# Another order for the float64 decoding inside the first MoE: ScalarE's copy one step later, and another list of units per slot

## The chip, the cores and the metric

The kernel runs on one core of one Trainium2 chip. The metric is device time in microseconds of one execution of the whole program; lower is better. Its engines each work through a queue of their own in the order in which the program lists their instructions: PE (matrix multiplies), ACT (ScalarE), DVE (VectorE), POOL (GpSimd) and SP (SyncE, which issues most of the DMAs). Semaphores hold an instruction back until what it reads has been written and what it overwrites is no longer needed.

## The reference

Attention with a learned position bias, then a mixture of eight experts (the first MoE), then a dense two-layer network (the second MoE). The change touches only the code around the last two:

```
# first MoE: each token goes to the expert with the largest logit
for e in range(E):                                   # E = 8, D = 512, F = 1024
    h = np.maximum(x[mask] @ w1[e], 0.0)
    out[mask] = gate_w[mask, None] * (h @ w2[e])
# second MoE: 2304 tokens, d_model 512, d_ff 2048; w_in and w_out are float64
h = x @ w_in
g = np.where(h > 0.0, h, alpha * (np.exp(np.minimum(h, 0.0)) - 1.0))
return (g @ w_out).astype(np.float32)
```

The weights of the second MoE arrive as float64, a format no engine multiplies. The kernel turns each number on the chip into two float32 parts, an upper one (`hi`) and the remainder (`lo`).

## The kernel before

Every product is made of three matrix multiplies of split operands: upper by upper, upper by lower, lower by upper. So each tile that PE produces in PSUM is read twice: ACT writes the upper part (`hTh`, `xTh`, `w1h`, `w2h`) and DVE subtracts it for the lower part (`hTl`, `xTl`, `w1l`, `w2l`).

The first MoE (`moe1`) goes through slots of up to 256 tokens of one expert. `slot(i)` takes one of two paths by the number of tokens in it. The full path (`layer1`) makes four groups `j` of 24 matmuls each; after each group ACT writes `hTh` and DVE `hTl` (lines 1146 and 1147). Then PE transposes the next slot's tokens (`x_transpose`, ACT `xTh` line 1074, DVE `xTl` line 1075) and runs the second layer (`layer2`, line 1188) for both halves of 128 tokens, whose output ACT scales into `y` (line 1195). The tail path (`layer1_tail`) is the same for at most 128 tokens, with `l1t` (line 1162), ACT `xgat` (line 1165) and the transposes `tph` (line 1173). Where the next slot belongs to another expert, `first_weights` (lines 1128 to 1132) splits its `w1` out of the staging tiles `stg` (ACT line 1103, DVE line 1108) and then loads its `w2` into the same tiles; `second_weights`, in the next slot, splits that `w2` and loads the following `w1`. The slots after the seventh run only while the tokens last; the sixteenth, called LAST, always runs.

Between these, the kernel decodes the float64 weights of the second MoE in 32 blocks. `decode_stages` gives the stages of a block: the load (line 1000, on SP), `magnitude` (ACT, line 1004), `upper` (two DVE instructions, lines 1007 and 1009, then ACT's copy to `hi`, line 1011), `lower` (four DVE instructions, lines 1014 to 1019) and `store` (SP, line 1025; only blocks 0 to 15, which are `w_out` and go back to DRAM; blocks 16 to 31 are `w_in` and stay in the tiles `wi`). `decode(u)` is one unit: for an even `u` it issues the lower parts of block `u/2 - 1`, the magnitude of block `u/2` and the load of block `u/2 + 2`; for an odd `u` the store of the block before and the upper part of its own. There are 66 units, 0 to 65. `UNITS` says how many each slot gets (slots 0 to 7, then LAST), and `units[i]` spreads them over eight places of a slot: `work(0)` to `work(2)` in the first layer, `work(3)` to `work(5)` after the transposes, before the second layer's first output, and `work(6)` and `work(7)` behind that output.

All queues but POOL's in the attention are written out in program order (`manual_schedule`), so the position of a unit in this code is its position on ACT, DVE and SP.

Of the kernel before, what the change touches and what calls it, by code (L numbers as in the profile page):

```python
# [40 lines left out]
DEC_W = 3  # L41
# [5 lines left out]
KVR = (1, 1, 2, 2, 2, 2, 2, 1, 1, 1, 1)  # L47
KVA = (2, 3)
OHE = ("vvv", "gvv", "gvg", "vvv")
UNITS = (0, 12, 12, 12, 10, 8, 12, 0, 0)  # L50
LAG = 1
OBUFS = 8
ROW = 520
# [111 lines left out]
class Kernel:  # L165
# [817 lines left out]
    def decode_stages(self, b):  # L983

        nc, V = self.nc, self.nc.vector  # L990
        w = self.dec_w[b % len(self.dec_w)]
        A = self.dec_m[b % len(self.dec_m)]
        r = self.dec_s[b % len(self.dec_s)]
        n = b % 16
        hi, lo = [t[:, :, 128 * n:128 * n + 128] for t in self.wi]
        v = lambda x: x.rearrange("p (k f) -> p k f", k=4)
        h, m = w[:, :, 1], w[:, :, 0]

        def load(eng=nc.sync):
            eng.dma_start(out=w.rearrange("p c w -> p (c w)"),  # L1000
                              in_=self.a["w64"][(b + 16) % 32].bitcast(I32))

        def magnitude():
            nc.scalar.activation(out=A, in_=h.bitcast(F32), func=AF.Copy, scale=2.0 ** -112)

        def upper():
            V.tensor_scalar(out=r.bitcast(I32), in0=A.bitcast(I32), scalar1=3, scalar2=0x7FFFF000,
                            op0=ALU.logical_shift_left, op1=ALU.bitwise_and)
            V.scalar_tensor_tensor(out=A.bitcast(I32), in0=A.bitcast(I32), scalar=self.dec_c[:, 0:1],  # L1009
                                   in1=r.bitcast(I32), op0=ALU.bitwise_and, op1=ALU.bitwise_or)  # L1010
            nc.scalar.activation(out=hi, in_=v(A), func=AF.Copy)

        def lower():
            V.tensor_scalar(out=r.bitcast(I32), in0=A.bitcast(I32), scalar1=self.dec_c[:, 1:2], scalar2=None,
                            op0=ALU.bitwise_and)
            V.tensor_scalar(out=m, in0=m, scalar1=9, scalar2=None, op0=ALU.logical_shift_right)
            V.scalar_tensor_tensor(out=m, in0=h, scalar=self.dec_c[:, 2:3], in1=m,  # L1017
                                   op0=ALU.logical_shift_left, op1=ALU.bitwise_or)
            V.scalar_tensor_tensor(out=lo, in0=v(m).bitcast(U32), scalar=2.0 ** -43, in1=v(r),  # L1019
                                   op0=ALU.mult, op1=ALU.mult)  # L1020

        def store():
            if b < 16:
                for j, x in enumerate((hi, lo)):
                    nc.sync.dma_start(out=self.wo_d[j, n].rearrange("p (k f) -> p k f", k=4), in_=x.bitcast(F32))

        return load, magnitude, upper, lower, store


    def moe1(self):  # L1030
        nc, tc, a, V = self.nc, self.tc, self.a, self.nc.vector
        with ExitStack() as es:
# [178 lines left out]
            dec = [self.decode_stages(b) for b in range(32)]  # L1211

            def decode(u):
                for first, stage in ((3, 4), (2, 3), (1, 2), (0, 1), (2 - 2 * DEC_W, 0)):
                    b, odd = divmod(u - first, 2)
                    if not odd and 0 <= b < 32 and (stage > 0 or b >= DEC_W):
                        dec[b][stage]()
# [6 lines left out]

            units, n = {}, 0
            for i, w in enumerate(UNITS):
                units[i] = lambda j, n=n, w=w: [decode(u) for u in range(n, n + w) if (u - n) * 8 // w == j]
                n += w

            def slot(i):  # L1230
                kind = reg(i, 1, 2)
# [425 lines left out]
```

## Time and profile before

| | |
|---|---|
| time, median of 3 runs | 1097.73 us (1094.53 to 1100.83) |
| the profiled execution | 1093.54 us, of which 1091.9 us are the span from the first to the last instruction |
| PE busy | 1035.2 us (95% of the span) |
| DVE busy | 702.0 us (64%) |
| ACT busy | 551.5 us (51%) |
| decoding, first to last magnitude | 422.8 to 581.5 us of the span |

The attention ends at about 375 us, the first MoE runs from there to 672.8 us, and the second MoE from there to the end. A busy PE here says little by itself: the records of matmuls overlap, so a stretch with waits shows best in how long a slot takes. In the rows below, "idle before" an instruction and the name behind the arrow say how long its engine stood and whose end it waited for.

### The profile page before, as it was taken

What the parts mean: (1) busy time and instruction counts of PE and PEld (TensorE: products, weight loads), DVE (VectorE), ACT (ScalarE), POOL (GpSimd) and SP (SyncE); (2) the same over time, 40 slices, a digit from 0 to 9 for tenths busy, and PEclk for the clock granted to TensorE, in tenths of its full rate; (3) what the DMA queues carried; (4) which work ended last, traced back from release to release, by engine and by line L of the source; (5) the groups of instructions that cost most, each with busy time, mean ns of one, the idle gap of its engine ahead of it and who ended that gap; (6) DMA issues with size and microseconds to landing.
All of it is one profiled execution on the core that took longest, in us unless ns stands there. A gap on an engine that the chain in (4) does not pass through costs nothing. (4 is left out here: it accounts for less than half of the span.)

```text
span 1091.9 us, 19524 instructions
## 1 busy us (share of the span) xinstructions
PE 1035.2 (95%) x6878; PEld 906.6 (83%) x6878; DVE 702.0 (64%) x1438; ACT 551.5 (51%) x1163; POOL 276.7 (25%) x437
## 2 busy tenths in 40 slices
PE   9999998999999989899899999999999999999996
PEld 3349988889998878777787888998989989899895
DVE  7779989989999895887887712533525335253350
ACT  7779877778787733444545513432424224242240
POOL 5646536665335343111211200000000000000000
PEclk9999999999999989999999999999999999999999
DMA  9985585764656477896744824600010100100000
GB/s 230 313 249 172 157 213 154 200 163 147 191 139 173 136 161 242 251 266 211 244 164 134 280 68 165 248 36 30 11 39 3 38 30 11 39 1 20 10 11 20
DMA packets 94566, 146.58 MB, mean 134 GB/s; under 512 B 11264, under 2 KB 53328, under 8 KB 94352
## 3 DMA queue, kind: packets, MB, share of 16 engines
q1 hardware_dynamic: 88976, 127.26, 39.8%
q0 software_dynamic: 5456, 17.70, 5.3%
q8 instruction: 64, 1.05, 0.4%
q14 instruction: 70, 0.57, 0.2%
HBM read 105.36 MB, written 36.70 MB: 130 GB/s over the span
## 5 line engine op out<-in xcount | busy, mean ns | idle before, releaser
L1415 PE MATMUL l1x<-xTl,wih 128*128 128x256 f32 x576 | 163.0, 283 | 0.0
L1415 PE MATMUL l1x<-xTh,wil 128*128 128x256 f32 x576 | 163.0, 283 | 0.0
L1415 PE MATMUL l1x<-xTh,wih 128*128 128x256 f32 x576 | 163.0, 283 | 0.0
L1423 DVE SCALAR_TENSOR_TENSOR t<-e,t 128x512 f32<-128x512 f32 x72 | 49.8, 692 | 132.8 <-ACT t L1422 132.8
L450 ACT ACTIVATE e<-s,mn 128x576 f32<-128x576 f32 x144 | 106.1, 737 | 33.1 <-DVE mn L440 26.8
L1439 POOL DMA_INDIRECT out<-y,idc x18 | 17.6, 979 | 395.2 <-ACT xTh L1404 271.3
L440 DVE CUSTOM_DVE_ANT_0 s<-s,bt 128x576 f32<-128x576 f32 x144 | 108.7, 755 | 7.3 <-PE s L429 4.3
L1434 PE MATMUL l2x<-woh,gTh 128*128 128x512 f32 x288 | 112.8, 392 | 0.0
L1434 PE MATMUL l2x<-wol,gTh 128*128 128x512 f32 x288 | 112.3, 390 | 0.0
L1434 PE MATMUL l2x<-woh,gTl 128*128 128x512 f32 x288 | 112.1, 389 | 0.0
L1415 PEld LDWEIGHTS l1x<-xTl,wih 128*128 128x128 f32 x576 | 110.6, 192 | 0.4
L1415 PEld LDWEIGHTS l1x<-xTh,wih 128*128 128x128 f32 x576 | 110.6, 192 | 0.4
L1415 PEld LDWEIGHTS l1x<-xTh,wil 128*128 128x128 f32 x576 | 110.6, 192 | 0.0
L1426 ACT ACTIVATE gTh<-t 128x512 fp32r<-128x512 f32 x72 | 45.5, 632 | 111.9 <-DVE t L1424 111.9
L429 PE MATMUL s<-ks,qh 128*128 128x288 f32 x320 | 92.7, 320 | 4.5 <-ACT e L450 4.4
L494 DVE TENSOR_TENSOR el<-t,eh 128x512 fp32r<-128x512 f32 x128 | 87.4, 683 | 2.8 <-DMA xgat<-in_kT 0.7
L463 PE MATMUL t<-ident,e 128*128 128x128 f32 x576 | 86.8, 273 | 0.5 <-DVE el L494 0.5
L1438 ACT ACTIVATE y<-l2x 128x512 f32<-128x512 f32 x18 | 10.8, 598 | 142.6 <-PE l2x L1434 142.6
L1427 DVE TENSOR_TENSOR gTl<-t,gTh 128x512 fp32r<-128x512 f32 x72 | 49.8, 692 | 50.4 <-ACT gTh L1426 50.4
L1188 PE MATMUL l2m<-w2h,hTl 128*128 128x512 f32 x168 | 69.9, 416 | 10.1 <-DVE hTl L1147 10.1
L487 ACT ACTIVATE eh<-t 128x512 fp32r<-128x512 f32 x128 | 75.2, 588 | 5.8 <-PE t L463 4.2
L1188 PE MATMUL l2m<-w2h,hTh 128*128 128x512 f32 x168 | 70.5, 419 | 5.8 <-ACT hTh L1146 5.6
(248 smaller groups left out, 2510.5 us busy)
## 6 DMA issues: line engine op xcount, KB each, us to landing
bt<-bias SPq DMA_DIRECT2D x32, 576.0 KB, 5.0
stg<-in_moe_w SPq DMA_DIRECT2D x32, 512.0 KB, 4.2
dec_w<-in_w SPq DMA_DIRECT2D x32, 512.0 KB, 5.4
bias<-o SPq DMA_DIRECT2D x36, 295.5 KB, 5.0
x_d<-y SPq DMA_DIRECT2D x22, 260.0 KB, 4.1
qraw<-in_qT SPq DMA_DIRECT2D x32, 160.0 KB, 3.7
k<-ks SPq DMA_DIRECT2D x32, 144.0 KB, 4.2
bt<-bias SPq DMA_DIRECT2D x32, 144.0 KB, 5.9
```

The lines of the kernel that those rows point to most:

```text
L429: nc.tensor.matmul(out=ps[:, half, 0:288], lhsT=x, rhs=k[:, half * 288:half * 288 + 288], start=(m == 0), stop=(m == len(seq) - 1))
L440: nc.vector.tensor_tensor_reduce(out=sc, in0=sc, in1=bt[:, t, :].rearrange("p (a k) -> p a k", a=2), scale=-0.125, scalar=3.0e38, op0=ALU. ...
L450: nc.scalar.activation(out=e.rearrange("p (a k) -> p a k", a=2), in_=T["ps"][:, :, 0:288], func=AF.Exp, scale=-1.0, bias=T["mn"], accum_ou ...
L463: nc.tensor.transpose(out=tp[:, c, :], in_=e[:, 128 * c:128 * c + 128], identity=ident)
L487: nc.scalar.activation(out=d["eh", T["b"]][:, 0:4, o:o + 128], in_=T["tp"], func=AF.Copy)
L494: nc.vector.tensor_tensor(out=d["el", bb][:, 0:4, o:o + n_], in0=src, in1=d["eh", bb][:, 0:4, o:o + n_].bitcast(F32), op=ALU.subtract)
L1188: nc.tensor.matmul(out=p, lhsT=hT[h][:, k, 128 * t:128 * t + 128], rhs=w2[wt][:, k, :], start=(k == 0 and h == wt), stop=(k == 7 and wt == 1))
L1415: nc.tensor.matmul(out=p[:, m, :], lhsT=wi[wt][:, k, ms], rhs=xT[x][:, k, :], start=(n == 0), stop=(n == 11))
L1423: V.scalar_tensor_tensor(out=t, in0=e, scalar=1.0, in1=t, op0=ALU.add, op1=ALU.mult)
L1426: nc.scalar.activation(out=gT[0][:, gs, :], in_=t, func=AF.Copy)
L1427: V.tensor_tensor(out=gT[1][:, gs, :], in0=t, in1=gT[0][:, gs, :].bitcast(F32), op=ALU.subtract)
L1434: nc.tensor.matmul(out=p, lhsT=gT[h][:, k, 128 * t:128 * t + 128], rhs=wo[wt][:, k, :], start=(n == 0), stop=(n == 47))
```

## The change

Two things. ACT's copy to `hi` leaves the stage `upper` and becomes a stage `high` of its own, which runs one unit later, ahead of `lower` of the same block. And the number of units is no longer spread evenly over eight places: `UNITS` lists them place by place. Slots 1 to 3 get 11 units where they had 12, slot 4 gets 8 (10), slot 5 8 (8), slot 6 10 (12), slot 7 4 (0) and LAST 3 (0). No slot has units at the places 6 and 7 any more.

```diff
-UNITS = (0, 12, 12, 12, 10, 8, 12, 0, 0)
+UNITS = ((), (2, 2, 1, 2, 2, 2), (2, 2, 1, 2, 2, 2), (2, 2, 1, 2, 2, 2), (2, 2, 0, 2, 1, 1), (0, 1, 1, 2, 2, 2),
+         (2, 2, 0, 2, 2, 2), (0, 2, 0, 2), (0, 1, 0, 2))
...
                                    in1=r.bitcast(I32), op0=ALU.bitwise_and, op1=ALU.bitwise_or)
+
+        def high():
             nc.scalar.activation(out=hi, in_=v(A), func=AF.Copy)
...
-        return load, magnitude, upper, lower, store
+        return load, magnitude, upper, high, lower, store
...
-                for first, stage in ((3, 4), (2, 3), (1, 2), (0, 1), (2 - 2 * DEC_W, 0)):
+                for first, stage in ((3, 5), (2, 3), (2, 4), (1, 2), (0, 1), (2 - 2 * DEC_W, 0)):
...
-                units[i] = lambda j, n=n, w=w: [decode(u) for u in range(n, n + w) if (u - n) * 8 // w == j]
-                n += w
+                units[i] = lambda j, n=n, w=w: [decode(n + sum(w[:j]) + u) for u in range(w[j] if j < len(w) else 0)]
+                n += sum(w)
```

How the queues move is shown at two places. First ACT's queue of the kernel before, from the end of slot 2 into slot 3. `wih` is the copy to `hi`, `dec_m` the magnitude, `y` an output of the second layer, and `hTh` the first group of slot 3.

```order
L1011 ACTIVATE wih<-dec_m_5738 128x4x128
L1004 ACTIVATE dec_m_5739<-dec_w_5736 128x512
L1011 ACTIVATE wih<-dec_m_5739 128x4x128
L1195 ACTIVATE y_70<-l2m,gate 128x512
L1048 TENSOR_LOAD tabi x2
L1255 COMPARE_AND_BRANCH
L1146 ACTIVATE hTh<-l_7198 128x512
```

The same place of the changed kernel, whose lines are numbered four higher:

```order
L1015 ACTIVATE wih<-dec_m_5737 128x4x128
L1006 ACTIVATE dec_m_5738<-dec_w_5735 128x512
L1259 UNCONDITIONAL_BRANCH
L1199 ACTIVATE y_70<-l2m,gate 128x512
L1052 TENSOR_LOAD tabi x2
L1259 COMPARE_AND_BRANCH
L1150 ACTIVATE hTh<-l_7206 128x512
```

Before, the copy of the block whose upper part DVE has last in its queue stands ahead of `y` and `hTh`; now the copy ahead of them is that of the block before, and the last upper part's copy comes in slot 3.

Second, DVE's queue in slot 7, tail path, of the kernel before, from the second `hTl` to the branch at the slot's end:

```order
L1177 TENSOR_TENSOR hTl<-tph,hTh 128x4x128
L1075 TENSOR_TENSOR xTl<-tp,xTh 128x4x128 x2
L1118 COMPARE_AND_BRANCH
L1108 TENSOR_TENSOR w1l<-stg_5726,w1h 128x4x256
L1108 TENSOR_TENSOR w1l<-stg_5727,w1h 128x4x256
L1108 TENSOR_TENSOR w1l<-stg_5728,w1h 128x4x256
L1108 TENSOR_TENSOR w1l<-stg_5729,w1h 128x4x256
L1118 UNCONDITIONAL_BRANCH x2
L1048 TENSOR_LOAD tabi
```

and of the changed kernel, from `xTl` to the third of the four `w1l`:

```order
L1079 TENSOR_TENSOR xTl<-tp,xTh 128x4x128 x2
L1009 TENSOR_SCALAR dec_s_5741<-dec_m_5739 128x512
L1011 SCALAR_TENSOR_TENSOR dec_m_5739<-dec_m_5739,dec_c,dec_s_5741 128x512
L1018 TENSOR_SCALAR dec_s_5741<-dec_m_5739,dec_c 128x512
L1020 TENSOR_SCALAR dec_w_5736<-dec_w_5736 128x512
L1021 SCALAR_TENSOR_TENSOR dec_w_5736<-dec_w_5736,dec_c 128x512
L1023 SCALAR_TENSOR_TENSOR wil<-dec_w_5736,dec_s_5741 128x4x128
L1122 COMPARE_AND_BRANCH
L1112 TENSOR_TENSOR w1l<-stg_5726,w1h 128x4x256
L1112 TENSOR_TENSOR w1l<-stg_5727,w1h 128x4x256
L1112 TENSOR_TENSOR w1l<-stg_5728,w1h 128x4x256
```

One decoded block now stands between the transposed tokens and the split of the next expert's first weights; a second one follows the split, ahead of the next slot's work.

## Rows read from the trace of the kernel before

**Rows 1.** The page, busy time of each engine.
```profile
PE 1035.2 (95%) x6878; PEld 906.6 (83%) x6878; DVE 702.0 (64%) x1438; ACT 551.5 (51%) x1163; POOL 276.7 (25%) x437
```

**Rows 2.** Slots 1 to 7 and LAST by windows: start:end, us, busy us of each engine (instructions).
```profile
core 0: us, PE busy (x) PEld busy (x) DVE busy (x) ACT busy (x) POOL busy (x), PEclk, DMA share, GB/s
419.00:442.17 23.17, 23.17 (x154) 21.25 (x153) 17.45 (x31) 9.88 (x17) 5.33 (x8) 1.00 0.74 229
442.17:470.97 28.80, 25.55 (x153) 22.29 (x152) 23.74 (x42) 11.63 (x20) 3.61 (x7) 0.94 0.87 269
470.97:497.32 26.35, 24.01 (x154) 21.09 (x152) 22.41 (x41) 10.22 (x19) 3.41 (x7) 1.00 0.90 265
497.32:526.01 28.69, 26.01 (x153) 22.03 (x152) 23.20 (x37) 13.42 (x21) 4.86 (x7) 0.94 0.61 181
526.01:557.21 31.20, 25.78 (x153) 21.90 (x152) 27.10 (x45) 14.62 (x24) 5.13 (x7) 0.95 0.71 245
557.21:581.69 24.48, 23.72 (x154) 21.17 (x153) 20.61 (x37) 10.21 (x19) 1.89 (x5) 1.00 0.35 123
581.69:594.98 13.29, 13.04 (x65) 10.69 (x64) 11.01 (x17) 9.24 (x14) 3.92 (x6) 1.00 0.31 102
...
659.20:672.77 13.57, 13.27 (x66) 10.92 (x67) 2.58 (x4) 3.26 (x6) 0.56 (x3) 1.00 0.44 140
```

**Rows 3.** PE in slot 5: start, us, instruction, [idle before, releaser].
```profile
544.67 0.80 PE L1188 MATMUL l2m<-w2h,hTl 128*128 128x512 f32 x1 [3.20 <-DVE hTl L1147]
```

**Rows 4.** Who waited for whom: us in total, times, longest.
```profile
ACT wih L1011 <- DVE dec_m L1009: 80.1, 30, 4.8
```

**Rows 5.** DVE in order of time, from slot 2's first hTl to slot 3's.
```profile
449.53 0.69 DVE L1147 SCALAR_TENSOR_TENSOR hTl<-l,hTh 128x512 fp32r<-128x512 f32 x1 [2.81 <-ACTq L1118]
...
455.02 0.69 DVE L1147 SCALAR_TENSOR_TENSOR hTl<-l,hTh 128x512 fp32r<-128x512 f32 x1 [1.18 <-ACT hTh L1146]
...
477.45 0.69 DVE L1147 SCALAR_TENSOR_TENSOR hTl<-l,hTh 128x512 fp32r<-128x512 f32 x1 [1.76 <-ACTq L1118]
```

**Rows 6.** ACT at the end of slot 2.
```profile
472.77 0.66 ACT L1004 ACTIVATE dec_m<-dec_w 128x512 f32<-128x512 f32 x1
475.73 0.64 ACT L1011 ACTIVATE wih<-dec_m 128x512 fp32r<-128x512 f32 x1 [2.29 <-DVE dec_m L1009]
```

**Rows 7.** DVE in slot 3: a hTl, a pair of xTl, then decoding.
```profile
489.89 0.68 DVE L1147 SCALAR_TENSOR_TENSOR hTl<-l,hTh 128x512 fp32r<-128x512 f32 x1
490.49 1.28 DVE L1075 TENSOR_TENSOR xTl<-tp,xTh 128x512 fp32r<-128x512 f32 x2
491.92 0.45 DVE L1007 TENSOR_SCALAR dec_s<-dec_m 128x512 int32<-128x512 int32 x1
...
495.45 0.42 DVE L1007 TENSOR_SCALAR dec_s<-dec_m 128x512 int32<-128x512 int32 x1
...
496.69 0.49 DVE L1014 TENSOR_SCALAR dec_s<-dec_m,dec_c 128x512 int32<-128x512 int32 x1
...
498.94 0.42 DVE L1007 TENSOR_SCALAR dec_s<-dec_m 128x512 int32<-128x512 int32 x1
```

**Rows 8.** DVE in slots 7 and 8.
```profile
590.12 1.28 DVE L1075 TENSOR_TENSOR xTl<-tp,xTh 128x512 fp32r<-128x512 f32 x2
591.50 4.63 DVE L1108 TENSOR_TENSOR w1l<-stg,w1h 128x1024 fp32r<-128x1024 f32 x4
599.76 2.36 DVE L1108 TENSOR_TENSOR w2l<-stg,w2h 128x1024 fp32r<-128x1024 f32 x2 [3.63 <-ACT w2h L1103]
```

**Rows 9.** ACT in slot 8.
```profile
598.03 0.60 ACT L1165 ACTIVATE xgat<-l1t 128x512 f32<-128x512 f32 x1 [2.02 <-PE l1t L1162]
```

**Rows 10.** PE's longest wait from 580 to 640 us: total, times, longest.
```profile
PE l2m L1188 <- DVE hTl L1147: 0.9, 1, 0.9
```

**Rows 11.** SP in slot 3, and a window of slot 2.
```profile
500.39 2.52 SPq L1025 DMA_DIRECT2D wo_d<-wih  x1
...
467.00:473.00 6.00, 6.00 (x37) 5.30 (x36) 5.79 (x11) 2.56 (x5) 0.00 (x0) 1.00 1.00 271
```

## Prediction

> **What bounds the kernel now.** I read the page first. PE is busy 95% of the span and DVE 64% [rows 1], so a gain has to come from places where PE stands, and the share of DVE says nothing of a single stage. The table by slots comes next, cut where PE starts a slot's first layer [rows 2]. Slot 1 has nothing to wait for: 23.17 us, PE busy from end to end. So this is what a full slot costs PE. Slots 2 to 6 have the same matmuls and take 28.80, 26.35, 28.69, 31.20 and 24.48 us, together 139.52 us against 5 x 23.17 = 115.85. The difference, 23.7 us, is all that a better order inside these slots can give. In the same rows DVE works 20.6 to 27.1 us per slot; the stage hangs on DVE, and on whom DVE waits for.
>
> Then PE's own waits: in slot 5 the second layer stood 3.20 us for a `hTl` of DVE [rows 3], and behind such a wait the clock fell: the granted clock of slots 2, 4 and 5 is 0.94 or 0.95, that of the others 1.00 [rows 2]. Last, who holds DVE up. ACT stood 80.1 us in front of `wih`, 30 times, for the upper part that DVE had just been given [rows 4]. ACT's queue is in order, so the next `hTh` stands behind that copy, and DVE's `hTl` waits for the `hTh`. DVE loses 1.18 us so in the middle of slot 2 and 1.76 us at the start of slot 3 [rows 5], where ACT's copy is free 2.29 us late [rows 6].
>
> **The change, part by part.** First DVE's prices [rows 7]. A `hTl` holds it 0.60 us (489.89 to 490.49), the pair of `xTl` 1.43 (to 491.92), an upper part 1.24 (495.45 to 496.69), the lower part 2.25 (to 498.94): one block, two units, 3.5 us. A full slot's own work is 4 x 0.60 + 1.43 = 3.83 us. For the kernel before this gives 6 x 3.5 + 3.83 + 1.18 + 1.76 = 27.8 us in slot 2; the two `hTl` at 449.53 and 477.45 are 27.9 apart [rows 5], so the list is complete to 0.1 us.
>
> *High one unit later.* It is the same instruction at the same price on ACT, which is half idle. The copy then waits for an upper part that lies a whole unit back on DVE, and where a place of the slot ends with an odd unit nothing of ACT waits at all. Where a place holds an odd and then an even unit, the copy still waits for DVE, but DVE then has 2.25 us of lower part to do, longer than copy and magnitude (0.64 and 0.66 us [rows 6]) and a `hTh` (some 0.6, as `xgat` [rows 9]) take together. So both of DVE's stalls go, 2.9 us a slot. What is late next is DVE's own turn at the slot's start, which no row separates from the 1.76 us: between 0 and 1.76, and I take 0.6, since most of that wait is ACT's chain of copy, `y` and `hTh`.
>
> *The new list.* DVE's work by slot: slot 2 has 6 upper and 5 lower parts, 18.7 + 3.8 = 22.5 us; slot 3 has 5 and 6, 19.7 + 3.8 = 23.5; slots 4 and 5 have 4 blocks, 14.0 + 3.8, and a split of weights each, 4.6 as in slot 7 [rows 8], 22.5; slot 6 has 5 blocks, 21.3. With 0.6 us per slot start that is 112.3 + 3.0 = 115.3 us for five slots, against PE's 115.85. The placement fits too: six units, 10.5 us, follow the transposes and run beside the second layer, and only five or fewer stand between the four `hTl`, of which the last is asked for when the second layer has three quarters of its first half behind it. PE is the bound again, with no margin: slot 3 is 1 us over its share, and in slot 5 the second split still stands ahead of three `hTl`. For these, and for loads that come late in slots 2 and 3, I add 2.6 us to the floor: 118.5 us. Gain 139.5 - 118.5 = 21.0 us. Bounds: 23.7 if no wait is left, and 12.2 if all stalls stay as they are and only the 7 units (3.5 blocks) that leave these slots count.
>
> *Slot 7's four units.* These cost. Slot 7 splits the first weights of the next expert, then loads its second ones into the freed staging tiles; slots 8 and 9 change experts again, and PE waits at most 0.9 us in that stretch [rows 10], so weights and PE run level and a delay is passed on. The first two units stand between `xTl` and the split: DVE's `w1l`, at 591.50 before [rows 8], starts 3.5 us later, and ACT's `w1h` with it, behind a copy that waits for DVE. The other two come after the split, in the old count at 591.5 + 3.5 + 4.6 = 599.6 us. ACT's copy there waits for an upper part until 600.9, and behind it stand copy, magnitude and `y`, some 0.65 us each, so the `xgat` of slot 8, at 598.03 before [rows 9], moves to 602.8. The `w2l` of slot 8 had 3.63 us of idle time before it [rows 8], which takes up part of the second block; it moves by 5 as `xgat` does. So slot 8 and the loads behind it come 5 us late. Bounds: 0, if the next weights had slack the rows don't show, and 7.0, both blocks in full.
>
> *LAST's three units* are one block, 3.5 us of DVE behind `xTl`. Before, DVE has only 2.58 us of work in that whole slot [rows 2], and the second MoE needs block 31 only in the last eighth of its first layer. I take 0; bound 3.5.
>
> Nothing of the load or store is added or taken; each DMA moves with its unit. Sum: -21.0 + 5.0 + 0 = -16.0 us. The profiled execution took 1093.5 us (span 1091.9), which would become 1077.5. It lies 4.2 us below the median of the runs shown, so against the median of 1097.7 I forecast 1081.7, **1081 us**.
>
> **The rivals.** (a) *The stalls stay.* ACT goes on holding DVE up at other places, and only the removed work counts: -12.2 + 5 = -7.2 us, 1090.5. For it: the odd-even places keep a wait of ACT for DVE. Against it: the list of DVE's time, complete to 0.1 us [rows 5 to 7], where both stalls have a named cause that goes. (b) *The DMA queues become the bound in slots 2 and 3.* They move 269 GB/s x 28.80 us = 7.7 MB in slot 2; less half a block (0.5 MB) in 23.2 us would need 310 GB/s. In six microseconds of slot 2 the share is full at 271 GB/s, and a store's issue was held 2.52 us in slot 3 [rows 11]. At 271 GB/s slot 2 takes 26.6 us, 3.4 more; slot 3, with 265 x 26.35 = 7.0 MB less the same, takes 24.0, what DVE takes anyway: -16.0 + 3.4 = -12.6, 1085.1. The Trainium skill (DMA: Bandwidth & Descriptors, Specifications) names 358 GB/s of HBM per core. By that rule 7.2 MB would take an estimated 20.1 us and this rival would fall; the full share at 271 GB/s in this trace speaks against the rule for these transfers. (c) *Slot 7's blocks are hidden*: -21, 1076.7. Against it stands only that PE and weights run level in slots 8 and 9. (d) *Slower.* Each `hTh` now stands behind a copy that waits for a whole block of DVE. If DVE falls one block (3.5 us) behind PE and stays there, PE waits that much in each of slots 2 to 6, and the clock falls behind each wait: 0.94 over 28.8 us is a loss of 1.7. Then 115.85 + 5 x 5.2 = 141.9 us, 2.3 above now, and slot 7 costs its full 7.0: +9.3, 1107. It decides from where DVE's work exceeds PE's 23.17 us in slot after slot; by the list above only slot 3 does, by 0.9.
>
> **How the numbers follow.** Chances: forecast 0.60 (1076 to 1084), (a) 0.14, (b) 0.12, (c) 0.08, (d) 0.06. What a measurement of this kernel can tell from no change is 0.5%, 5.5 us. The forecast, (c) and nearly all of (b) are faster than that; (a) lies on the edge, half of it within. So faster 0.86, same 0.08, slower 0.06. The forecast's bounds, -23.7 to -1.7 with all costs at their ends, are 1074 to 1096; with the spread of the runs (3 us to each side) and (a) inside I give 1071 to 1093.
>
> **What would show it.** Right: ACT's wait before the copy to `hi` falls far below 80 us in total; slots 2 to 6 take 23 to 25 us each with a granted clock of 1.00; slot 7's first matmul comes near 560 us; the stretch from there to the second MoE's first matmul grows from 91.1 us (581.69 to 672.77) to about 96 [rows 2], with PE waiting at `tph` or in the second layer of slots 8 and 9. Wrong: slots 2 and 3 with a DMA share of 1.00 and ACT waiting for `dec_w` (rival b); `hTl` still waiting for `hTh` in the full slots (a, d); a stretch after slot 7 as long as now (c), or longer by more than 7 us, where LAST's block would be found.

## The result, and the profile after

The changed kernel takes 1079.69 us (median of four runs, 1077.34 to 1081.36) against 1096.13 us of the kernel before on the same chip: ratio 0.9865, 95% interval 0.9834 to 0.9896, a gain of 16.4 us by the medians. The forecast was 1081 us, a gain of 16.0, with a range of 1071 to 1093. The profiled execution took 1077.34 us, its span 1075.7 us, 16.2 us less than before.

The instructions are as many as before [rows 1]; PE is busy 7.8 us less for the same 6878 matmuls, DVE and ACT 2 us more:

```profile
PE 1027.4 (96%) x6878; PEld 904.2 (84%) x6878; DVE 704.0 (65%) x1438; ACT 553.2 (51%) x1163; POOL 277.9 (26%) x437
```

The windows from one slot's first matmul to the next one's, slots 1 to 8 and LAST, with the columns of [rows 2] (the last one runs 0.1 us past LAST's end):

```profile
419.71:442.88 23.17, 23.17 (x153) 21.25 (x152) 17.85 (x32) 9.35 (x16) 6.12 (x13) 1.00 0.85 267
442.88:466.01 23.13, 23.13 (x153) 21.25 (x152) 21.12 (x37) 10.47 (x18) 3.42 (x7) 1.00 0.85 270
466.01:490.84 24.83, 23.76 (x153) 21.11 (x152) 21.38 (x39) 10.97 (x20) 3.91 (x7) 1.00 0.89 292
490.84:514.18 23.34, 23.34 (x153) 21.18 (x152) 21.73 (x35) 12.78 (x21) 4.23 (x7) 1.00 0.80 243
514.18:540.00 25.82, 24.04 (x153) 21.01 (x152) 21.87 (x35) 12.82 (x21) 4.07 (x7) 1.00 0.75 254
540.00:563.16 23.16, 23.16 (x153) 21.20 (x152) 21.44 (x38) 10.68 (x19) 1.39 (x5) 1.00 0.48 156
563.16:577.67 14.51, 13.49 (x65) 10.46 (x64) 11.08 (x19) 8.81 (x15) 2.89 (x3) 1.00 0.50 155
577.67:592.50 14.83, 12.05 (x50) 9.52 (x51) 13.63 (x18) 10.64 (x16) 8.26 (x11) 0.88 0.74 242
643.37:656.90 13.53, 13.23 (x65) 10.88 (x66) 5.93 (x10) 3.90 (x7) 0.56 (x3) 1.00 0.44 141
```

Slots 2, 4 and 6 now take what PE needs, 23.1 to 23.3 us, and the granted clock of slots 2 to 6 is 1.00 everywhere. Slots 2 to 6 sum to 120.28 us (139.52 before), a gain of 19.2. Slot 8, cut short in this window, lasts to 595.71 (18.04 us, before 13.53), at a granted clock of 0.88 in its first 14.8 us. From slot 7's first matmul to the second MoE's first (656.79) it is 93.63 us, before 90.92 (581.69 to 672.61): 2.7 us given back. The other 0.3 us lie ahead of slot 2 (+0.7) and behind the first MoE (-0.4).

Part of the gain is the clock. Before, the granted clock was 0.50, that is 1.2 GHz where 1.00 is 2.4, for 3.4 us each in slots 2, 4 and 5, from 462.67, 517.28 and 544.59 us on, each time from the end of a wait of PE's. The changed kernel has no such stretch in slots 2 to 6 and one in slot 8, after a wait of 1.72 us. The third of before, after the 3.20 us of [rows 3], and the one after:

```profile
544.59:548.00 3.41, 3.33 (x7) 2.12 (x8) 2.19 (x6) 2.23 (x5) 0.00 (x0) 0.50 0.95 350
```

```profile
587.27:590.68 3.41, 3.41 (x15) 3.22 (x16) 3.41 (x4) 3.41 (x6) 2.36 (x2) 0.50 0.57 155
```

At half the clock 3.4 us do the work of 1.7; by this estimate some 5 of the 19.2 us are the clock, and 1.7 of the 4.5 us that slot 8 lost.

PE's remaining waits in the full slots (start, us, instruction, [idle before, releaser]) are one in slot 3 and two in slot 5, where the longest was 3.20 us [rows 3]:

```profile
483.41 0.50 PE L1192 MATMUL l2m<-w2h,hTh 128*128 128x512 f32 x1 [0.85 <-ACT hTh L1150]
...
528.72 0.50 PE L1192 MATMUL l2m<-w2h,hTl 128*128 128x512 f32 x1 [0.52 <-DVE hTl L1151]
533.29 0.50 PE L1192 MATMUL l2m<-w2h,hTl 128*128 128x512 f32 x1 [1.20 <-DVE hTl L1151]
```

ACT's waits between 415 and 680 us (total, times, longest). The copy to `hi` still waits 67.1 us, against 80.1 [rows 4]:

```profile
ACT wih L1015 <- DVE dec_m L1011: 67.1, 28, 4.0
...
ACT dec_m L1006 <- DMA dec_w<-in_w: 5.4, 4, 2.1
```

What fell is DVE's wait for `hTh`, before and after, from 415 to 600 us:

```profile
DVE hTl L1147 <- ACT hTh L1146: 10.0, 8, 1.8
```

```profile
DVE hTl L1151 <- ACT hTh L1150: 1.3, 2, 0.7
```

DVE's `hTl`, the four of slot 2 and the first of slot 3. The wait in the middle of slot 2 is gone; the one at slot 3's start is not, 1.91 us where it was 1.76 [rows 5]:

```profile
446.80 0.69 DVE L1151 SCALAR_TENSOR_TENSOR hTl<-l,hTh 128x512 fp32r<-128x512 f32 x1 [1.05 <-ACTq L1122]
451.14 0.68 DVE L1151 SCALAR_TENSOR_TENSOR hTl<-l,hTh 128x512 fp32r<-128x512 f32 x1
455.24 0.68 DVE L1151 SCALAR_TENSOR_TENSOR hTl<-l,hTh 128x512 fp32r<-128x512 f32 x1
456.96 0.68 DVE L1151 SCALAR_TENSOR_TENSOR hTl<-l,hTh 128x512 fp32r<-128x512 f32 x1
...
472.19 0.69 DVE L1151 SCALAR_TENSOR_TENSOR hTl<-l,hTh 128x512 fp32r<-128x512 f32 x1 [1.91 <-ACT dec_m L1006]
```

ACT just before that last one. What holds it is no longer the copy, but a block that comes late from DRAM, and two `y` in a row:

```profile
466.18 0.64 ACT L1015 ACTIVATE wih<-dec_m 128x512 fp32r<-128x512 f32 x1 [1.49 <-DVE dec_m L1011]
468.36 0.67 ACT L1006 ACTIVATE dec_m<-dec_w 128x512 f32<-128x512 f32 x1 [1.54 <-DMA dec_w<-in_w]
468.94 1.26 ACT L1199 ACTIVATE y<-l2m,gate 128x512 f32<-128x512 f32 x2
470.08 0.60 ACT L1150 ACTIVATE hTh<-l 128x512 fp32r<-128x512 f32 x1
```

In slots 7 and 8 ACT and then DVE show the two blocks. Counted from slot 7's first matmul, `w1l` starts 13.56 us in (before 9.81), `xgat` 21.03 (16.34) and `w2l` 22.76 (18.07) [rows 8, 9]: 3.8, 4.7 and 4.7 us later.

```profile
575.57 3.90 ACT L1107 ACTIVATE w1h<-stg 128x1024 fp32r<-128x1024 f32 x4 [0.39 <-SPq L1122]
582.52 0.64 ACT L1015 ACTIVATE wih<-dec_m 128x512 fp32r<-128x512 f32 x1 [3.05 <-DVE dec_m L1011]
...
584.19 0.60 ACT L1169 ACTIVATE xgat<-l1t 128x512 f32<-128x512 f32 x1
```

```profile
576.72 4.63 DVE L1112 TENSOR_TENSOR w1l<-stg,w1h 128x1024 fp32r<-128x1024 f32 x4 [0.41 <-ACT w1h L1107]
...
585.92 2.36 DVE L1112 TENSOR_TENSOR w2l<-stg,w2h 128x1024 fp32r<-128x1024 f32 x2 [1.06 <-ACT w2h L1107]
```

One thing the prediction did not look at: SP's queue. The two `y` of a slot go to the same DRAM tensor, and the second store waits on SP until the first has landed (`DMA x_d<-y` in the rows below). SP's waits of that kind from 415 to 600 us, before and after:

```profile
SPq L1199 <- DMA x_d<-y: 5.7, 5, 2.1
```

```profile
SPq L1203 <- DMA x_d<-y: 24.3, 6, 4.6
```

Before, decoding at places 6 and 7 stood between the two `y`. In the new list nothing does, and both come at once. SP in slot 3 after (the pair of stores, then the next load of a block), and ACT, where that load's block is awaited ahead of the `hTh` for which PE waits 0.85 us:

```profile
470.51 6.04 SPq L1203 DMA_DIRECT2D x_d<-y  x2
478.50 0.34 SPq L1002 DMA_DIRECT2D dec_w<-in_w  x1
```

```profile
482.20 0.67 ACT L1006 ACTIVATE dec_m<-dec_w 128x512 f32<-128x512 f32 x1 [1.06 <-DMA dec_w<-in_w]
482.78 0.58 ACT L1150 ACTIVATE hTh<-l 128x512 fp32r<-128x512 f32 x1
```

### The profile page after: what moved, and what is told of

It is laid out like the page before. It is cut to its first block, busy times and chain, and to the rows that moved or that the text cites. A ratio compares the mean times of both kernels' runs of the same rounds, so it can differ in the third digit from the quotient of the medians.

```text
span 1075.7 us, 19524 instructions
## 1 busy us (share of the span) xinstructions
PE 1027.4 (96%) x6878; PEld 904.2 (84%) x6878; DVE 704.0 (65%) x1438; ACT 553.2 (51%) x1163; POOL 277.9 (26%) x437
## 3 DMA queue, kind: packets, MB, share of 16 engines
q8 instruction: 64, 1.05, 0.4%
## 5 line engine op out<-in xcount | busy, mean ns | idle before, releaser
L431 PE MATMUL s<-ks,ql 128*128 128x288 f32 x256 | 72.5, 297 | 0.0
L465 PEld LDWEIGHTS t<-ident,e 128*128 128x128 f32 x576 | 71.1, 141 | 0.7 <-ACT eh L489 0.6
```

Of the source, the lines that this page charges most:

```text
L431: nc.tensor.matmul(out=ps[:, half, 0:288], lhsT=x, rhs=k[:, half * 288:half * 288 + 288], start=(m == 0), stop=(m == len(seq) - 1))
L465: nc.tensor.transpose(out=tp[:, c, :], in_=e[:, 128 * c:128 * c + 128], identity=ident)
```

## The experiments

All in one table: us per slot from the first matmul of each slot, as above; "2 to 6" their sum; "7 on" from slot 7's first matmul to the second MoE's first. The instructions ahead of slot 1 are the same in all of these kernels, and yet slot 1 begins between 414.35 and 423.98 us in these profiles. So the medians tell kernels a few us apart only roughly, and the slots, most of which come out within 0.8 us in the repeats, tell where. Slot 8 differs by 1.1 us between the two profiles of e7: one has 3.4 us at a granted clock of 0.50 there, the other none.

| kernel | median us | ratio (95%) | 2 | 3 | 4 | 5 | 6 | 2 to 6 | 7 | 8 | 9 | 10 | LAST | 7 on |
|---|---|---|---|---|---|---|---|---|---|---|---|---|---|---|
| before | 1096.13 | 1 | 28.80 | 26.35 | 28.69 | 31.21 | 24.47 | 139.52 | 13.29 | 13.53 | 25.73 | 24.96 | 13.41 | 90.92 |
| changed | 1079.69 | 0.9865 (0.9834-0.9896) | 23.13 | 24.83 | 23.34 | 25.82 | 23.16 | 120.28 | 14.51 | 18.04 | 23.13 | 24.53 | 13.42 | 93.63 |
| e1_copy_only | 1080.22 | 0.9879 (0.9846-0.9912) | 23.44 | 25.53 | 23.14 | 30.33 | 23.14 | 125.58 | 13.29 | 13.51 | 25.09 | 25.11 | 13.44 | 90.44 |
| e2_list_only | 1084.31 | 0.9919 (0.9886-0.9951) | 24.79 | 30.31 | 23.14 | 25.98 | 23.14 | 127.36 | 14.54 | 18.04 | 23.17 | 24.76 | 13.63 | 94.14 |
| e3_counts_only | 1084.40 | 0.9922 (0.9895-0.9949) | 27.21 | 27.17 | 23.14 | 29.28 | 23.14 | 129.94 | 13.65 | 17.63 | 23.17 | 24.90 | 13.87 | 93.22 |
| e4_slot7_to_last | 1080.56 | 0.9897 (0.9866-0.9928) | 23.14 | 24.62 | 23.44 | 25.31 | 23.16 | 119.67 | 14.69 | 16.16 | 23.68 | 24.89 | 17.77 | 97.19 |
| c0_changed | 1077.09 | 0.9868 (0.9839-0.9897) | 23.13 | 25.17 | 23.50 | 25.13 | 23.15 | 120.08 | 14.56 | 17.88 | 23.14 | 24.75 | 13.43 | 93.76 |
| e5_last_pair_behind | 1073.80 | 0.9826 (0.9797-0.9856) | 23.13 | 23.19 | 23.18 | 25.11 | 23.14 | 117.75 | 14.01 | 17.97 | 23.36 | 24.58 | 13.54 | 93.46 |
| e6_slot5_late | 1078.07 | 0.9871 (0.9843-0.9899) | 23.14 | 25.52 | 23.44 | 23.50 | 25.51 | 121.11 | 14.60 | 16.78 | 23.17 | 24.65 | 13.41 | 92.61 |
| e7_both | 1070.07 | 0.9813 (0.9779-0.9847) | 23.13 | 23.51 | 23.19 | 23.16 | 24.01 | 117.00 | 14.00 | 17.09 | 23.17 | 24.57 | 13.41 | 92.24 |
| e7_again | 1072.81 | 0.9809 (0.9783-0.9836) | 23.13 | 23.43 | 23.13 | 23.67 | 24.78 | 118.14 | 14.02 | 18.23 | 23.14 | 24.49 | 13.43 | 93.31 |
| e8_second_block | 1075.47 | 0.9843 (0.9813-0.9874) | 25.13 | 24.29 | 23.60 | 23.16 | 24.08 | 120.26 | 14.01 | 15.22 | 25.95 | 24.45 | 13.42 | 93.05 |
| e9_slot7_free | 1073.91 | 0.9825 (0.9799-0.9851) | 25.42 | 24.81 | 23.18 | 23.17 | 24.18 | 120.76 | 13.30 | 13.50 | 23.85 | 24.50 | 14.18 | 89.33 |
| e10_early_copy | 1079.44 | 0.9879 (0.9850-0.9908) | 25.28 | 27.89 | 23.71 | 23.17 | 24.20 | 124.25 | 14.01 | 17.06 | 23.56 | 25.05 | 13.40 | 93.08 |

e1 to e4 shared runs of the kernel before with a median of 1092.37 us, c0 to e7_both 1091.79, e7_again to e10 1091.62.

### The two halves of the change

**e1_copy_only**: `high` as in the change, the old list spread evenly.

```diff
-UNITS = ((), (2, 2, 1, 2, 2, 2), ...
+UNITS = (0, 12, 12, 12, 10, 8, 12, 0, 0)
```

> Only the copy is moved; the list of units is the old one (12, 12, 12, 10, 8, 12, spread over eight places). Theory (both parts count, the copy ends DVE's two stalls of 2.9 us a slot): the stalls are what is left of the 21.0 us when the 12.2 us of removed work are taken off, 8.8 us, so about 1087 us against 1096 of before, with slots 2 and 3 at 25 to 26 us. Rival 1 (the copy's place is worth nothing, since ACT still waits 67.1 us for upper parts in the changed kernel): 1096. Rival 2 (the copy is the whole gain of slots 2 to 6): 1096 - 19 = 1077, since slot 7 is spared.

Slots 2 to 6 fell by 13.9 us, much more than the 8.8 of the theory and less than the 19.2 of the second rival, since slot 5 hardly moved; the first rival falls. The total, 0.9879, lies between the theory and the second rival. The windows of slots 2 to 6:

```profile
444.91:468.35 23.44, 23.43 (x153) 21.17 (x152) 21.79 (x39) 10.48 (x19) 3.66 (x7) 1.00 0.99 308
468.35:493.88 25.53, 23.73 (x153) 21.17 (x152) 23.87 (x43) 11.53 (x21) 4.26 (x7) 1.00 0.95 291
493.88:517.02 23.14, 23.14 (x154) 21.25 (x152) 22.09 (x36) 13.29 (x22) 5.67 (x7) 1.00 0.70 216
517.02:547.35 30.33, 26.61 (x154) 23.25 (x153) 28.85 (x48) 15.66 (x25) 6.10 (x7) 0.89 0.74 249
547.35:570.49 23.14, 23.14 (x154) 21.25 (x153) 20.33 (x36) 10.18 (x18) 1.32 (x5) 1.00 0.40 144
```

With all 12 units slot 2 takes 23.44 us and slot 4 23.14: the sum of DVE's work in a slot, 24.8 us by the prediction's prices, was no floor there. DVE did 21.8 of it within the slot; the rest ran into later ones. What is left over comes due in slot 5, where DVE also has the split, is busy 28.85 us with 48 instructions (35 in the changed kernel), and PE waits 1.05 and 2.67 us and runs at half the clock for 6.8 us from about the end of the second wait.

**e2_list_only**: the copy directly behind its upper part, the new list.

```diff
         def upper():
             ...
+            nc.scalar.activation(out=hi, in_=v(A), func=AF.Copy)
         def high():
-            nc.scalar.activation(out=hi, in_=v(A), func=AF.Copy)
+            pass
```

> The new list of units, but the copy to hi directly behind its upper part as before. Theory (both parts count): the stalls come back where a place holds an even and then an odd unit (slot 2's second half, slot 3's first half, slot 6), so 3 to 9 us above the changed kernel: 1083 to 1089. Rival (the new list begins most places with an odd unit, where the copy's old and new place are the same on the queue; so the list alone does it): 1080, slots 2 and 6 at 23.2 us each.

7.1 us more than the changed kernel in slots 2 to 6, all of it in slots 2 and 3 (1.7 and 5.5), the other slots to 0.2 us as there. That is the theory in size, but the places are not quite the ones it names: the copy stands elsewhere where an odd unit is the last before other work. A place with an even and then an odd unit is one such case, where other work follows it; another is an odd unit with a place to itself, as in slot 2, between the third `hTl` and the fourth. There the copy holds the fourth `hTh`, DVE stands 1.18 us as it did before in mid-slot [rows 5], and PE waits 0.79 us:

```profile
459.44 0.69 DVE L1152 SCALAR_TENSOR_TENSOR hTl<-l,hTh 128x512 fp32r<-128x512 f32 x1 [1.18 <-ACT hTh L1151]
```

Slot 6 has no such place, so the expectation of a stall there was wrong. ACT in slot 3 (the copy for DVE, then `hTh`), and PE's wait for it, from about the end of which the granted clock is 0.50 for 6.8 us, by the estimate above 3.4 of slot 3's 5.5 us:

```profile
484.69 0.63 ACT L1013 ACTIVATE wih<-dec_m 128x512 fp32r<-128x512 f32 x1 [3.58 <-DVE dec_m L1011]
485.22 0.58 ACT L1151 ACTIVATE hTh<-l 128x512 fp32r<-128x512 f32 x1
```

```profile
485.85 0.80 PE L1193 MATMUL l2m<-w2h,hTh 128*128 128x512 f32 x1 [3.09 <-ACT hTh L1151]
```

**e3_counts_only**: new numbers per slot, evenly spread, the copy early.

```diff
+UNITS = (0, 11, 11, 11, 8, 8, 10, 4, 3)
```

> Only the numbers per slot are the new ones (11, 11, 11, 8, 8, 10, 4, 3); the units are spread evenly over eight places and the copy stands where it was. Theory (removed work counts 12.2 us, slot 7's units cost the 2.5 us that the changed kernel shows): 1096 - 9.7 = 1086. Rival 1 (only the sum per slot matters, DVE being below PE's 23.17 us in each slot): 1080, as the changed kernel. Rival 2 (places matter, counts don't: the units between the hTl hold PE's second layer up as before): 1093 to 1096.

Slots 2 to 6 gained 9.6 us (theory 12.2), 7 on lost 2.3. Total 0.9922, 8.5 us of 1092.4, near the theory's 9.7. Slots 2, 3 and 5 still wait, so sums per slot are not all. (The execution profiled here took 1090.85 us, 6.5 above the median, and its slot 1 begins 5.0 us later than that of the kernel before.) The parts do not add up: 9.6 for counts, 12.2 for the list (counts and places), 13.9 for the copy, 19.2 for list and copy. List and copy overlap by 6.9 us: in part they remove the same waits.

### What slot 7 costs

**e4_slot7_to_last**: slot 7's four units in LAST.

```diff
-         (2, 2, 0, 2, 2, 2), (0, 2, 0, 2), (0, 1, 0, 2))
+         (2, 2, 0, 2, 2, 2), (), (0, 2, 2, 3))
```

> The changed kernel with slot 7's four units moved into LAST, which then has seven. Theory (slot 7's blocks delay the splits of the next weights by 2.5 us net, and LAST's DVE, busy 5.9 of 13.5 us, takes another 7 us beside PE): slot 7 to the second MoE 91 us again instead of 93.6, 1077 us. Rival 1 (LAST's blocks then stand in front of DVE's first work of the second MoE, or its first layer wants block 30 before it is there): 1080 to 1084. Rival 2 (the 2.5 us come from the loads of the weights, which start no earlier, and not from the units): 1080 as now.

This is not the theory: slot 7 takes 14.69 us without any unit in it. LAST pays 4.35 us for seven units, PE waiting 2.19 us at 656.27 to read a `hTl`, with DVE's decoding (L1020) named as what it waited for, and the total is no better (0.9897). The second rival comes nearest: the loads start no earlier (below). What slot 7 waits for, ACT names:

```profile
573.94 3.90 ACT L1107 ACTIVATE w1h<-stg 128x1024 fp32r<-128x1024 f32 x4 [3.87 <-SPq L1122]
```

By this row ACT's `w1h` waits for SP to reach the same branch (L1122). SP had issued the first of the two `y` stores at 566.46 and the second only at 571.48. So there were two causes for slot 7's lateness, and taking one away left the other.

**c0_changed** is the changed kernel again, beside the next three.

> The changed kernel itself, on the same chip as the next three, to compare them with. All theories: 0.985 to 0.988 of the kernel before; slots 2 to 6 23.1, 24.8, 23.3, 25.8 and 23.2 us, slots 7 and 8 14.5 and 18.0.

As expected; slots 3 and 5 differ by 0.3 and 0.7 us from the first profile.

**e5_last_pair_behind**: the last units of slots 1 to 6 behind the first `y` (slots 1 to 3 shown).

```diff
-(2, 2, 1, 2, 2, 2)
+(2, 2, 1, 2, 2, 0, 2)
```

> The changed kernel with the last units of slots 1 to 6 moved from place 5 to place 6, behind the first of the two outputs y. Theory (in the changed kernel both y of a slot come at once behind the decoding, the second one's store waits on SP for the first to land, 24.3 us in six slots, and SP is late for the next load in slot 3 and for the branch in slot 7, on which ACT's w1h waits): SP's wait falls below 10 us, slot 3 takes under 24.2 us instead of 24.8, slots 7 and 8 together under 31 instead of 32.5; 2 to 3 us less than the changed kernel. Rival 1 (slots 7 and 8 are late because of slot 7's own four units): 14.5 and 18.0 stay, no difference. Rival 2 (units between the two y hold up the second y and the hTh behind it): slots 2 to 6 a microsecond longer each, 3 to 5 us more than the changed kernel.

SP's wait fell to 9.6 us and slot 3 to 23.19, both as the theory has it; 3.3 us less than c0 by the medians, 2.6 by the slots from 2 on. The total alone does not show it, its interval overlaps c0's. ACT's wait for `dec_w` up to 600 us fell from 5.4 us in the changed kernel (5.9 in c0) to 0.2. Slots 7 and 8 gained only 0.5 together, so for these the first rival is right: `w1h` no longer waits for SP there (575.22, no idle time before it), and the units decide. SP's waits, and SP in slot 3, where a load now goes between the two stores:

```profile
SPq L1203 <- DMA x_d<-y: 9.6, 6, 2.4
```

```profile
469.82 0.47 SPq L1203 DMA_DIRECT2D x_d<-y  x1
471.43 0.33 SPq L1002 DMA_DIRECT2D dec_w<-in_w  x1
...
475.77 0.36 SPq L1203 DMA_DIRECT2D x_d<-y  x1
```

**e6_slot5_late** and **e7_both**:

```diff
-(0, 1, 1, 2, 2, 2)
+(0, 0, 0, 2, 2, 4)       # e6
+(0, 0, 0, 2, 2, 0, 4)    # e7, with e5's other places
```

> The changed kernel with slot 5's two units of the places 1 and 2 moved to place 5, so that nothing of the decoding stands between the split of the second weights and the last three hTl. Theory (in slot 5 the split of 4.7 us and these units stand ahead of the hTl for which PE waits 0.52 and 1.20 us): slot 5 takes 23.2 to 24.2 us instead of 25.8, slot 6 stays under 23.6; 1.5 to 2.5 us less than the changed kernel. Rival (the hTl are late because ACT's w2h waits 2.83 us for SP's queue, so the units don't matter): slot 5 25 us or more, no difference.

Slot 5 fell to 23.50 us, so the two units between the split and the `hTl` were most of its price (ACT's `w2h` still waits 2.36 us there, so the rival falls), but slot 6 rose to 25.51: four units ahead of the `y` pair moved the delay on. No gain.

> Both of these edits. Theory: they add up, 4 to 5 us less than the changed kernel, about 1075 us. Rival (four units in one place at the end of slot 5 hold the last y and slot 6's first hTh, or the stores now collide with the loads): 0 to 2 us less.

With the four units behind the first `y`, slot 5 takes 23.16 and slot 6 24.01: 3.1 us less than c0 in slots 2 to 6. The medians say 7.0 us on this chip; the slots account for 4.6, and for 2.4 in the repeat.

> e7_both once more, on the same chip as the next three. All theories: 0.979 to 0.984 of the kernel before; slots 7 and 8 14.0 and 17.1 us, slots 9 and 10 23.2 and 24.6.

0.9809 (0.9783 to 0.9836): the lowest ratio, below the kernel before by 1.9% and below the changed kernel by about half a per cent. The intervals of e5 and e9 overlap it, so that it is the best of them is not shown.

**e8_second_block** and **e9_slot7_free**, from e7:

```diff
-(2, 2, 1, 2, 2, 0, 2)  slot 1;  (0, 2, 0, 2) slot 7;  (0, 1, 0, 2) LAST
+(2, 2, 2, 2, 2, 0, 3)  slot 1;  (0, 2)       slot 7;  (0, 1, 0, 2) LAST    # e8
+(2, 2, 2, 2, 2, 0, 3)  slot 1;  ()           slot 7;  (0, 2, 0, 3) LAST    # e9
```

> e7_both with slot 7's second two units (place 3, behind the split of the weights) moved to slot 1, which then has 13, as (2, 2, 2, 2, 2, 0, 3); the units of all later slots come two earlier, with the same places. Theory (slot 8's xgat stands on ACT behind a copy that waits 3.1 us for the block behind the split, and PE waits 0.5 and 1.7 us for it): slot 8 falls from 17.1 to 14 to 15 us, slots 9 and 10, which wait for loads again, give 1 to 2 us of it back, the sum is 1 to 1.5 us under e7; slot 1 stays at 23.2. Rival 1 (slot 8 is late because of w1l, which stands behind the first block): slot 8 stays at 16.5 to 17. Rival 2 (two more units in slot 1 put DVE behind, and slot 2 takes 1 to 3 us more): above e7.

Slot 8 fell by 3.0 us against e7_again, and slot 9 rose by 2.8: over the stretch the second block costs nothing that the repeats could tell (93.05 against 93.31 and 92.24). Slot 2 rose by 2 us (the second rival), so slots 2 to 6 take 2.1 us more than in e7_again; in the total the intervals overlap.

> e7_both with no unit in slot 7: two more in slot 1 (13), two more in LAST (5, as (0, 2, 0, 3)). Theory: slots 7 and 8 take 13.3 and 13.5 us as in the kernel before, slots 9 and 10 25.1 each, so that of the 3.7 to 4.3 us that slots 7 and 8 win about 2.5 are given back; LAST, which cost 4.3 us with seven units and nothing with three, costs 1 to 2 with five. About the same as e7. Rival (slot 7's blocks cost 5 us net as predicted): 3 us or more under e7.

Slots 7 and 8 are back at 13.3 and 13.5 us, and 7 on takes 89.33, 4.0 us under e7_again although LAST pays 0.75 for five units. For that stretch the rival is right: without the first block, and with the stores apart as in e7, it is 2.9 to 4.0 us shorter. The windows of slots 7 to 9:

```profile
564.53:577.83 13.30, 13.05 (x66) 10.70 (x64) 10.37 (x16) 9.18 (x14) 3.84 (x6) 1.00 0.46 145
577.83:591.33 13.50, 13.25 (x65) 10.62 (x64) 9.34 (x10) 8.83 (x13) 5.33 (x8) 1.00 0.87 290
591.33:615.18 23.85, 23.46 (x153) 21.17 (x152) 12.26 (x13) 11.49 (x15) 4.44 (x8) 1.00 0.81 280
```

The time is lost again in slots 2 and 3 (25.42 and 24.81), as slot 2 was in e8, so the total is not under e7's.

One number tells these kernels apart in two groups: when the first of the four loads behind the `w1l` of slot 7 is issued, from slot 7's first matmul. SP in e9, 11.0 us in:

```profile
575.54 3.78 SPq L1097 DMA_DIRECT2D stg<-in_moe_w  x4
```

It is 11.1 us in the kernel before and in e1, 14.8 in the changed kernel (units and SP), 15.0 in e4 (SP alone), 14.3 in e5, e7_again and e8 (units alone), 11.0 in e9 (neither). From there to slot 10's first matmul it is 39.5 to 41.5 us in all eight, and in the other six as well, whatever slot 8 does between. Inside a group, this spread of 2 us decides.

**e10_early_copy**: e7 with the edit of e2.

> e7_both with the copy to hi back behind its upper part. Theory (the copy's place matters only where an even and then an odd unit share a place: slot 2's second half, slot 3's first half, now also the pair at place 6 of slots 2 and 3): slots 2 and 3 together 5 to 8 us longer, the other slots as in e7. Rival (with the y pair apart the copy's place no longer matters): no difference.

Slots 2 and 3 take 53.17 us instead of 46.56, 6.6 more, the others as in e7 to 0.6 us: the theory. The copy's place matters in e7's list too.

## Why the prediction was right, point by point

**The bound.** Right: the gain lay in slots 2 to 6, in waits for `hTh` and `hTl`, and the clock rose with them to 1.00. 118.5 us were forecast there, 120.3 came, and slot 7's first matmul came at 563.2 instead of near 560. The allowance of 2.6 us over PE's floor was too small: 4.4 remained, nearly all in slots 3 and 5, the two that it was meant for. That the total came out to half a us is in part luck: 1.8 us too much gain here and 2.3 too much cost behind slot 7 nearly cancel.

**The high stage.** Right in kind: without it (e2, e10) the copy holds `hTh` again, 6.6 to 7.1 us in slots 2 and 3. Alone it gave 13.9 us, not the 8.8 of e1's expectation. The prediction set a slot's DVE work against PE's time slot by slot; e1 shows that work in excess of a slot can run into the next, as long as the `hTl` are served in time, and that what is left over comes due later, there in slot 5. Of the two stalls only the one in mid-slot went. At the slot's start 1.91 us stayed where 0.6 were allowed, with another cause (a late block, two `y`).

**The new list.** Right that it helps; what it is worth hangs on the copy. In slots 2 to 6 it gave 12.2 us without the copy moved (e2) and 5.3 on top of it (125.58 to 120.28), 4.5 of these in slot 5, where the half clock goes too. Behind slot 7 it costs 3.2 us on top of the copy (90.44 to 93.63). So in the whole program the copy alone does nearly all: 0.9879 in e1 against 0.9865 and 0.9868, which these intervals do not tell apart. The prediction's bound of 12.2 counts seven units, but only six leave slots 2 to 6 (10.5 us at its price); the seventh leaves slot 1, and counts as far as slot 1's excess runs into slot 2, as e8 shows it does. Slot 5's rest was placed rightly (split and units ahead of the `hTl`: e6, e7). For slot 3 the prediction named DVE's one us too much and late loads; its 1.7 us came from late loads, and e5 shows that these came from SP, which the list had left without work between the two stores.

**Slot 7's units.** The term that was off: +5.0 forecast, +2.7 measured. `w1l`, `xgat` and `w2l` came as late as forecast (3.8, 4.7, 4.7 us), and slots 7 and 8 took 5.7 us more. The step that failed is "so weights and PE run level and a delay is passed on", and with it "so slot 8 and the loads behind it come 5 us late": the loads go out right behind `w1l`, so only 3.8 late, and the second block runs beside them, which e8 shows. Slots 9 and 10, which had 25.73 and 24.96 us where a full slot needs 23.2, gave 3.0 us back; [rows 10] shows only the longest of PE's waits, not what these slots lost. Also, the units were not the only cause; SP alone makes the loads as late (e4). What the units alone cost is told by e7 against e9, both with the stores apart: 2.9 to 4.0 us, or 3.7 to 4.7 if the 0.75 that LAST pays in e9 is left out. That is nearer to 5.0 than 2.7 is, and the kernel before, with 90.92 us against 89.33 in e9, was not at its floor.

**LAST.** Right: 13.42 us against 13.41. Five units cost 0.75, seven 4.35.

**The rivals.** (a) fell: DVE's wait for `hTh` went from 10.0 to 1.3 us, and e1 and e2 show the copy's part in it. (b) fell: slot 2 took 23.13 us, e1's slot 2 moved 308 GB/s in 23.44, and from 466 to 472 us the queues moved 375 GB/s, so the full share at 271 GB/s was no ceiling. The kernel before could have told, six us of its slot 5 moved 393 GB/s:

```profile
526.00:532.00 6.00, 6.00 (x52) 5.99 (x51) 5.75 (x12) 2.36 (x4) 0.00 (x0) 1.00 1.03 393
```

The rule quoted from the Trainium skill (DMA: Bandwidth & Descriptors, Specifications), 358 GB/s for a core, was the better guide here, and in these six us the traces lie above it. Rival (c) fell by 2.7 us, (d) with slots 2 to 6.

**The signs.** The stretch behind slot 7 grew, to 93.6 us where about 96 were forecast, with PE waiting 1.72 us at `tph` in slot 8, as said; slots 2 to 6 kept to their 23 to 25 us but for slot 5 (25.8). One sign was ill chosen. ACT's wait before the copy was to fall far below 80 us; it is 67.1, or 65.0 to 600 us, and 79.1 to there in e2, whose slots 4 to 6 take what they take in the changed kernel. In these queues, worked through in order, a wait cost only where something needed stood behind it.

## What to carry to other kernels

Before moving work between places of a queue, list for each place what stands directly behind it on every engine, the queue that issues DMAs included: taking the work out from between two stores to one tensor made the second wait for the first, and the engine that issues the loads stood 24 us. Judge an in-order engine's work by whether the next needed result comes in time, not by its sum per stage, and a wait by who is queued behind it. Add up the parts of a change only where they remove different waits. Where one cause is taken away and nothing moves, look for a second that is just as late before calling the first harmless.

## What the runs showed of the hardware

The share and the rate of the DMA engines do not go together: share 1.00 at 271 GB/s before [rows 11], 0.99 at 308 GB/s over all of slot 2 in e1, and 375 GB/s at 1.09 in the window of the changed kernel that is shown here. (A share can pass 1, since a packet's whole time counts where it starts.)

```profile
466.00:472.00 6.00, 6.00 (x52) 5.98 (x51) 3.60 (x7) 4.16 (x8) 0.00 (x0) 1.00 1.09 375
```

A store of 260 KB to DRAM and the next one to the same tensor were issued 5.0 us apart (566.46 and 571.48 in e4), 3.8 of which SP waited for the first.

The granted clock fell to 0.50 at the end of waits of PE's: 3.20 us in slot 5 before, 1.72 in slot 8 after, 2.67 in slot 5 of e1, 3.09 in slot 3 of e2. It did not at every wait: slot 6 of e6 waited 1.02 and 0.76 us and stayed at 1.00.

Open stay why the way from the loads in slot 7 to slot 10 takes 39.5 us in e4 and e9 and up to 41.5 in others, why ACT waits at a branch for SP, and why slot 6 takes 24.0 to 24.8 us in e7. A list with e7's places, slot 7 free and slot 1 unchanged was not tried.
